# Holding batch 1's V, its spreads and its global casts behind batch 0's copies of V, and counting instruction fetches longer, in a planned attention and MoE kernel

## The chip, the core and the metric

The kernel runs on one core of one Trainium2 chip. A core has TensorE (PE, matmuls; PEld is its weight load), VectorE (DVE), ScalarE (ACT), GpSimd (POOL) and SyncE (SP), each with an instruction queue of its own that runs in order, and 16 DMA engines that all queues share. SP, ACT and POOL issue transfers; one that changes the type of its data is issued by POOL. The metric is device time in microseconds (us) of a whole execution; the median of three runs of the kernel before is 330.26 us (330.26 to 330.88).

## The reference

Eight batches of attention with eight heads of 64, a local part of 512 tokens with a band of 32 to each side, and 32 global tokens; then a two-layer MoE expert on all 4352 rows.

```
k_all = concat(k_g, k_l);  v_all = concat(v_g, v_l)
out_g = softmax(q_g k_all' / 8) v_all                     # 32 global rows see all 544 keys
s_ll  = where(|i - j| <= 32, q_l k_l' / 8, -1e9)          # local rows see a band
out_l = softmax(concat(q_l k_g' / 8, s_ll)) v_all         # and the 32 global keys
x     = concat(out_g, out_l), heads side by side          # 4352 x 512
h     = x @ w_in                                          # 512 -> 2048
out   = (h * clip(h + 3, 0, 6) / 6) @ w_out               # 2048 -> 512, float32
```

## The kernel before

**A planner writes the order.** Every piece of work is an `Op` with its engines and their estimated costs, the operations that it depends on, and the buffers that it takes and frees. It stands in a named stream; within a stream the order is fixed. `Plan.lay` (L123) keeps a clock for each engine and lays, step by step, the operation that can start first; among those that can start on one engine within 0.03 us the lowest rank of its stream wins. An operation with a choice of engines goes to the one on which it ends first. The order that comes out is what each engine's queue executes; on the chip only semaphores hold an engine. So a changed rank or cost moves instructions, and nothing else.

**Instruction fetches.** The planner counts PE instructions in blocks of 256 (`BLOCK`, L43). When PE passes a block's edge, the next block is taken to arrive at `fetched` (L180): 3.4 us later, and up to 3.0 us more where the DMA clock lies ahead. An operation that would run into a block not yet there gets 20 added to its rank (L147), so that others go first.

**Attention of a batch.** `loads` (L407) brings q and k, `g_first` (L461) the global q and k of batches 0 and 1, `v_loads` (L536) V. `turn_qk` (L597) transposes them on DVE (`qt`, `kt`; L609, L614, L624), after which small copies called halos (L631, stream "kg", on POOL or ACT) repeat edge columns. `local` (L697) makes a pair of 32-row windows of all heads, four pairs a batch: scores on PE (L731 or, from batch 2 on, L718), mask and maximum on DVE (L762), exponential on ACT (L768), turning on PE (L777), its copy out of PSUM (L319 on ACT, L321 on DVE), the product with V on PE (L795), normalising and transposing on DVE (L804, L805, L818). `globe` (L822) does the same for the global rows (L843, L850, L855, L866, L876).

**Copies of V.** The product with V needs the rows of V shifted by 32 and beside the global rows of V. `v_loads` loads V into `v0` and shifts it with copies within the chip ("strips", L538 to L568, stream "vs"): about 29 for batch 0, on POOL, ACT or DVE; ten for each later batch, on POOL alone. The global V is loaded into `vg` by `vg_load` (L517) and repeated into `vs` by four transfers of SP (`spread`, L526). `made["strips"]` keeps batch 0's strips.

**The global q and k** go as FP32 into a staging tile and are cast into `gn0`. For batch 0, `once` (L486) loads 32 rows once and casts them four times into four quarters of the partitions. For batch 1, `g_first` loads them four times for q and four times for k (eight transfers of SP into `graw`) and casts each in one instruction (L479, ACT or DVE).

**The MoE.** `moe_first` (L971) multiplies by `w_in` (L926), gates on ACT and DVE (L937, L933); `moe_second` (L992) multiplies by `w_out` (L953), copies out (L961) and stores by SP. Batch 0's first layer goes in parts of 128, 128 and 256 columns (`PARTS`). The attention of batch b lies beside the MoE of batch b - 1. `w_out` comes in four transfers of POOL, `load_w_out` (L588).

**Order of the loads.** All transfers of stream "l0" keep their order on POOL: batch 0's, `w_in`, batch 1's q and k, batch 1's global V and V, `w_out`, then batch 2's q and k (`rawq`, `rawk`). Further, the planner lets no engine have more than eight transfers under way (`LANES`, L98).

Of the kernel before, what the change touches and what calls it, by code (L numbers as in the profile page):

```python
# [9 lines left out]
FP32 = mybir.dt.float32  # L10
# [27 lines left out]
class Plan:  # L38
# [5 lines left out]
    FETCH = 3.4  # L44
    COLD, SLOW = 30.0, 1.9
    SWITCH, ALONE = 0.097, 0.0
    SPARE, PHASES = 0.4, 9
# [75 lines left out]
    def lay(self):  # L123
        at = self.at = {n: 0 for n in self.streams}
        clock = {}
        order = []
        total = sum(len(s) for s in self.streams.values())
        while len(order) < total:
# [46 lines left out]
            if e == "PE":  # L175
                wait, when = self.stalls(op, start, self.cost(op, e, start))
                end += wait
                self.mode = op.mode[1]
                if self.count % self.BLOCK + op.n >= self.BLOCK:
                    self.fetched = when + wait + self.FETCH + min(3.0, max(0.0, clock.get("DMA", 0.0) - when - 0.5))  # L180
                self.count += op.n
# [12 lines left out]
def kernel(  # L194
# [12 lines left out]
    nc = tc.nc  # L207
# [51 lines left out]
    graw = tiles("graw", 2, [P, NC, D], FP32)  # L259
# [37 lines left out]
    for name, rank in (("l0", 0), ("ld", 5), ("lq", -2), ("sh", 0), ("sq", 0), ("st", 2), ("g0", 0), ("ga", -9), ("first", -9), ("pad", -30), ("gc", -6), ("gd", 3), ("cast", -5), ("msk", lambda n: 1 if n < 9 else 1.25), ("tq", lambda n: 0 if n < 8 else 3), ("kg", -1), ("vs", 2.2), ("clr", 1),  # L297
                       ("s", 0.5), ("mx", lambda n: 1.2 if n < 33 else 2.7), ("ex", 1.2), ("t", -0.5), ("etc", 0), ("av", -0.7), ("nm", 1.5),
                       ("xp", -0.5), ("gx", 1),
                       ("mf", lambda n: 9 + n * 1e-3), ("ms", lambda n: 9 + (n + len(PARTS) * NDFF + 2) * 1e-3), ("t1", 0), ("gate", -0.7), ("ot", 0)):  # L300
        plan.stream(name, rank)
# [159 lines left out]
    def g_first(b):  # L461

        after = [w_in_l[1][1]] if b else []
        state[b]["gl"] = {}
        for k, src, name in ((1, k_g, "k"), (0, q_g, "q")):
            if b == 0:
                once(k, src, name)
                continue
            rows = src[b].rearrange("(c e) g d -> e g c d", e=2)
            g, w, got = Buf("gn" + name, 1), Buf("gr" + name, 1), []  # L470
            state[b]["gn", k] = g
            for e in range(2):
                for f in range(2):
                    got.append(load("sh" if b else "ga" if k else "g0", "SP" if b or not k else "ACT", 0.47, 0.2, graw[k][quarter(e, f)], rows[e], after, () if got else [w]))

            def cast(engine, k=k):
                o, i = (t[k].rearrange("p c d -> p (c d)") for t in (gn0, graw))
                if engine == "ACT":
                    nc.scalar.copy(out=o, in_=i)  # L479
                else:  # L480
                    nc.vector.tensor_copy(out=o, in_=i)
            op = Op({"ACT": 0.37, "DVE": 0.3}, None, got, [g], [w])
            op.emit = lambda op=op, cast=cast: cast(op.engine)
            state[b]["gl"][k] = [plan.add("gc", op)]

    def once(k, src, name):  # L486

        raw_ = ots[k][0:W].rearrange("g (h d) -> g h d", d=D)
        got = load("ga", "ACT", 0.47, 0.3, raw_, src[0].rearrange("h g d -> g h d"))
        state[0]["gn", k] = Buf("gn" + name, 1)  # L490
        state[0]["gl"][k] = []
        for e in range(2):
            for f in range(2):
                def cast(engine, e=e, f=f):
                    o, i = gn0[k][quarter(e, f)], raw_.rearrange("g (c e) d -> g e c d", e=2)[:, e]
                    if engine == "ACT":
                        nc.scalar.copy(out=o, in_=i)
                    else:
                        nc.vector.tensor_copy(out=o, in_=i)
                op = Op({"ACT": 0.37, "DVE": 0.3} if k else {"ACT": 0.37}, None, [got], [state[0]["gn", k]] if not state[0]["gl"][k] else [])  # L500
                op.emit = lambda op=op, cast=cast: cast(op.engine)
                state[0]["gl"][k].append(plan.add("gc" if k else "gd", op))
# [23 lines left out]
    def spread(b, units_, after):  # L526
# [3 lines left out]
        for u in units_:  # L530
            a = ORDER[u].index("g") * W
            st["vs"][u, 0] = [load("sh", "SP", 0.5, 0.3, lambda u=u, a=a: vs[v.slot][a:a + W, u],
                                lambda: vg[v.slot][0:W].rearrange("p (j h) d -> p j h d", j=1).to_broadcast([W, NJ, H, D1]), [after], lat=2.0 + LATE[b])]
            st["vs"][u, 1] = list(st["vs"][u, 0])

    def v_loads(b, to):  # L536
# [6 lines left out]
        vl = [load(to, "POOL", 0.8, 1.05 if b else 1.25, lambda j=j: v0[v.slot][:, j, :, 0:D],  # L543
                   v_l[b, :, j * P:(j + 1) * P, :].rearrange("h s d -> s h d"), lat=LATE[b] if b else 3.3 - 0.4 * j) for j in range(NJ)]

        def shift(u, z, n, src, js, dj, need):
# [8 lines left out]
            op = Op({"POOL": c, "ACT": c, "DVE": c if n == W else 1.35 * c} if b == 0 else {"POOL": c}, None, [vl[j + dj] for j in js])  # L555
# [457 lines left out]
    with tc.manual_schedule():  # L1013
# [14 lines left out]
        w_out_l = load_w_out()  # L1028
        for b in range(2, B):
# [23 lines left out]
        moe_second(B - 1, NJ - 1, 2)  # L1053
        for need, op in made["strips"]:
# [41 lines left out]
```

## Time and profile before

| | |
|---|---|
| median of three runs | 330.26 us |
| the profiled execution's own time | 331.21 us |
| its span, first to last instruction | 329.4 us |
| busy: PE, DVE, ACT, POOL | 306.1, 259.6, 236.7, 154.7 us |
| PE busy from 0 to 16 us, 16 to 24, 24 to 44 | 6.45, 4.20, 15.80 us |
| PE busy from 44 to 56 us, 56 to 96, 96 to 226 | 11.74, 39.16, 130.00 us |
| mean granted clock of TensorE | 0.988 |

A PE that counts as busy is not at its peak, since the ends of matmuls are modelled; an idle PE, though, is idle. A wait is told as the engine and line that waited, and what released it; "issue" is a wait for nothing that the profile shows. In the timeline a row gives the start, the length, what ran, how many, and in brackets the idle time before it and what ended that.

### The profile page before, as it was taken

What the parts mean: (1) busy time and instruction counts of PE and PEld (TensorE: products, weight loads), DVE (VectorE), ACT (ScalarE), POOL (GpSimd) and SP (SyncE); (2) the same over time, 40 slices, a digit from 0 to 9 for tenths busy, and PEclk for the clock granted to TensorE, in tenths of its full rate; (3) what the DMA queues carried; (4) which work ended last, traced back from release to release, by engine and by line L of the source; (5) the groups of instructions that cost most, each with busy time, mean ns of one, the idle gap of its engine ahead of it and who ended that gap; (6) DMA issues with size and microseconds to landing.
All of it is one profiled execution on the core that took longest, in us unless ns stands there. A gap on an engine that the chain in (4) does not pass through costs nothing.

```text
span 329.4 us, 11223 instructions
## 1 busy us (share of the span) xinstructions
PE 306.1 (93%) x4484; PEld 172.8 (52%) x4484; DVE 259.6 (79%) x916; ACT 236.7 (72%) x545; POOL 154.7 (47%) x201
## 2 busy tenths in 40 slices
PE   4457889999989999999999999999999999999995
PEld 3336786555545555555554554554455545556653
DVE  7789996898878898989899899898898874672210
ACT  7869668757977798769867987589758796553221
POOL 9998299409995802993249519923800000000000
PEclk9977999999999999999999999999999999999999
DMA  8999999999952996299969991998211012101222
GB/s 199 186 207 193 206 210 113 176 251 162 191 106 66 157 178 124 47 134 180 211 88 147 169 131 34 120 190 145 62 39 34 2 34 67 32 2 33 65 57 72
DMA packets 105429, 39.67 MB, mean 120 GB/s; under 512 B 92256, under 2 KB 98144, under 8 KB 105376
## 3 DMA queue, kind: packets, MB, share of 16 engines
q0 software_dynamic: 91392, 16.91, 65.8%
q1 hardware_dynamic: 13440, 21.91, 28.2%
q8 instruction: 35, 0.57, 0.7%
q10 hardware_dynamic: 544, 0.13, 0.2%
q14 instruction: 18, 0.15, 0.1%
HBM read 35.26 MB, written 8.91 MB: 134 GB/s over the span
## 4 chain that ended last, share of the span: by engine, by line
PE 76%; POOL 9%; issue 6%; DVE 4%; ACT 2%; DMA 1%; SPq 0%; POOLq 0%
PE m L953 32%; PE m L926 31%; PE t L777 3%; POOL vs L561 3%; PE a L795 3%; PE s L718 2%; POOL v L309 2%; DMA rawq<-rawq 1%; PE s L835 1%; PE t L866 1%; PE a L876 1%; DVE gts L933 1%; PE s L731 1%; DVE x L805 1%; PE m L731 1%
## 5 line engine op out<-in xcount | busy, mean ns | idle before, releaser
L953 PE MATMUL m<-wout,gts 128*128 128x512 f16 (+1 forms) x560 | 131.8, 373 | 0.0
L926 PE MATMUL m<-xt,win 128*128 128x512 f16 (+2 forms) x640 | 121.6, 339 | 3.3 <-DVE gts L933 3.3
L933 DVE SCALAR_TENSOR_TENSOR gts<-t,m 128x512 f16<-128x512 f32 x136 | 92.0, 681 | 30.5 <-ACT t L937 29.0
L937 ACT ACTIVATE t<-m 128x512 f32<-128x512 f32 x136 | 80.8, 596 | 43.4 <-PE m L926 41.2
L561 POOL COPY vs<-v 32x1056 f32<-32x1056 f32 (+5 forms) x87 | 79.4, 912 | 48.9 <-DMA v<-in_v_l_dram 44.8
L926 PEld LDWEIGHTS <-win 128*128 128x128 f16 x704 | 70.7, 114 | 49.6 <-issue 4.9
L768 ACT ACTIVATE ex<-sm,mx 128x128 f16<-128x128 f32 x256 | 86.3, 395 | 10.1 <-DVE mx L762 9.5
L953 PEld LDWEIGHTS <-gts 128*128 128x128 f16 x560 | 51.2, 98 | 49.8 <-issue 2.4
L762 DVE CUSTOM_DVE_ANT_0 sm<-s,mask 128x128 f32<-128x128 f32 x240 | 56.2, 284 | 8.1 <-PE s L731 3.2
L961 ACT COPY ot<-m 128x512 f32<-128x512 f32 (+1 forms) x35 | 20.0, 572 | 12.6 <-PE m L953 12.6
L319 ACT COPY et<-t 128x1024 f16<-128x1024 f16 x26 | 26.2, 1006 | 3.3 <-PE t L777 3.1
L309 POOL DMA_DIRECT2D v<-in_v_l_dram x32 | 28.2, 900 | 0.0
L309 POOL DMA_DIRECT2D rawq<-in_q_l_dram x12 | 12.6, 1056 | 23.9 <-DVE qt L665 13.0
L805 DVE TENSOR_TENSOR x<-a,rec 128x512 f16<-128x512 f32 x32 | 22.1, 692 | 1.1
L818 DVE STREAM_TRANSPOSE xt<-x 128x512 f16<-128x512 f16 x32 | 22.4, 701 | 0.2
L762 DVE DVE_READ_ACCUMULATOR2_ANT mx<- 128x1 f32 x256 | 21.2, 83 | 0.0
L777 PEld LDWEIGHTS <-ex 128*128 128x128 f16 x256 | 17.4, 102 | 6.3 <-issue 0.4
L777 PE MATMUL t<-ident,ex 128*128 128x128 f16 x240 | 19.2, 225 | 0.0
L795 PEld LDWEIGHTS <-et 128*32 128x32 f16 x1024 | 10.0, 97 | 14.1 <-ACT ex L768 3.8
L665 DVE STREAM_TRANSPOSE qt<-rawq 128x512 f16<-128x512 f16 x24 | 15.8, 687 | 0.6 <-DMA rawq<-rawq 0.6
L795 PE MATMUL a<-vs,et 128*32 128x65 f16 x1024 | 14.2, 196 | 2.0 <-ACT et L319 1.1
L319 ACT COPY etg<-t 128x640 f16<-128x640 f16 x15 | 10.4, 693 | 7.6 <-PE t L866 7.5
(93 smaller groups left out, 220.4 us busy)
## 6 DMA issues: line engine op xcount, KB each, us to landing
out_dram<-ot SPq DMA_DIRECT2D x62, 128.0 KB, 2.4
vs<-vg SPq DMA_DIRECT2D x32, 132.0 KB, 7.6
v<-in_v_l_dram POOLq DMA_DIRECT2D x32, 128.0 KB, 9.1
rawq<-in_q_l_dram POOLq DMA_DIRECT2D x12, 256.0 KB, 5.8
rawk<-in_k_l_dram POOLq DMA_DIRECT2D x12, 256.0 KB, 7.6
rawq<-rawq SPq DMA_DIRECT2D x12, 254.0 KB, 7.1
rawk<-rawk SPq DMA_DIRECT2D x12, 254.0 KB, 7.5
win<-in_moe_w_in_dram POOLq DMA_DIRECT2D x4, 512.0 KB, 10.3
```

The source lines that it names most:

```text
L309: eng.dma_start(out=o() if callable(o) else o, in_=i() if callable(i) else i)
L319: nc.scalar.copy(out=o(), in_=i())
L561: (nc.gpsimd if op.engine == "POOL" else nc.vector).tensor_copy(out=o(), in_=i())
L762: nc.vector.tensor_tensor_reduce(out=sms[sm.slot], in0=scored(c // 2)[:, z:z + P], in1=mask(m), scale=-scale, scalar=3.0e38, op0=ALU.add, ...
L768: nc.scalar.activation(out=exs[ex.slot][:, un, c, :], in_=sms[sm.slot], func=EXP, scale=-1.0, bias=mxs[mx.slot])
L777: nc.tensor.matmul(out=turned(tp)[:, z:z + P], lhsT=exs[ex.slot][:, un, c, :], rhs=ident, is_transpose=True)
L795: nc.tensor.matmul(out=o[hq * W:(hq + 1) * W, 4 * f + 2 * un + kh, 0:D + 1], lhsT=ets[et.slot][:, un, c, quarter(e, f) if b >= WORDS else ...
L805: nc.vector.tensor_tensor(out=xs[x.slot].rearrange("p g (a d) -> p g a d", a=2), in0=o[:, :, 0:D].rearrange("p g (d a) -> p g a d", a=2), ...
L926: nc.tensor.matmul(out=mps[ps.slot][:, k * n:(k + 1) * n], lhsT=column_tile(c)[:, m], rhs=x, start=(m == 0), stop=(m == KC - 1))
L933: nc.vector.scalar_tensor_tensor(out=g, in0=shape(t1s[t1.slot][:, 0:all_]), scalar=1.0, in1=shape(mps[ps.slot][:, 0:all_]), op0=ALU.min, o ...
L937: r = plan.add("t1", Op(("ACT", 0.09 + all_ * 0.00083), lambda: nc.scalar.activation(out=t1s[t1.slot][:, 0:all_], in_=mps[ps.slot][:, 0:al ...
L953: nc.tensor.matmul(out=mps[ps.slot][:, 0:n], lhsT=gfn(c), rhs=w_out_t[c // 4][:, c % 4, cols], start=(c == 0), stop=(c == NDFF - 1))
```

## The change

It has six parts. (1) Batch 1's load of the global V may be laid on POOL only after the last of batch 0's strips has been laid (`holds`); what follows it in its stream (batch 1's V, `w_out`, batch 2's loads) follows it here too. (2) Batch 1's four spreads depend on the third transfer of `w_out`. (3) Batch 1's global q and k go the way of batch 0's: one transfer each into a new tile `graw0`, and four casts each, in a new stream "gp", on POOL or ACT. (4) The fetch of a block is counted as 7.0 us from a start before 40 us and as 5.2 us later, whatever the DMA clock. (5) Ranks: "kg" from -1 to 0.5, "vs" from 2.2 to 1.5, "ex" from 1.2 to 1.9, "nm" from 1.5 to 0.7, "st" from 2 to 3.5, "ot" from 0 to 3; `ALONE` and `SPARE` to 0.5. (6) Costs: strips of batch 0 on POOL and ACT, casts, V's issue, spreads.

```diff
-    FETCH = 3.4
-    SWITCH, ALONE = 0.097, 0.0
-    SPARE, PHASES = 0.4, 9
+    SWITCH, ALONE = 0.097, 0.5
+    SPARE, PHASES = 0.5, 9
...
-                    self.fetched = when + wait + self.FETCH + min(3.0, max(0.0, clock.get("DMA", 0.0) - when - 0.5))
+                    self.fetched = when + wait + (7.0 if when < 40.0 else 5.2)
...
-    graw = tiles("graw", 2, [P, NC, D], FP32)
+    graw0 = tiles("graw0_", 1, [W, 2, H, D], FP32)[0]
...
-    ("st", 2), ... ("kg", -1), ("vs", 2.2), ... ("ex", 1.2), ... ("nm", 1.5), ... ("ot", 0)
+    ("st", 3.5), ... ("gp", 3.9), ... ("kg", 0.5), ("vs", 1.5), ... ("ex", 1.9), ... ("nm", 0.7), ... ("ot", 3)
...
     def g_first(b):
-        after = [w_in_l[1][1]] if b else []
         state[b]["gl"] = {}
         for k, src, name in ((1, k_g, "k"), (0, q_g, "q")):
-            if b == 0:
-                once(k, src, name)
-                continue
-            rows = src[b].rearrange("(c e) g d -> e g c d", e=2)
...
-                    got.append(load("sh" if b else "ga" if k else "g0", "SP" if b or not k else "ACT", 0.47, 0.2, graw[k][quarter(e, f)], rows[e], after, () if got else [w]))
...
-            op = Op({"ACT": 0.37, "DVE": 0.3}, None, got, [g], [w])
...
+            once(b, k, src, name)
-    def once(k, src, name):
+    def once(b, k, src, name):
+        raw_ = (graw0[:, k] if b else ots[k][0:W].rearrange("g (h d) -> g h d", d=D))
+        got = load("sh" if b else "ga", "SP" if b else "ACT", 0.47, 0.45 if b else 0.3, raw_, src[b].rearrange("h g d -> g h d"), [w_in_l[1][1]] if b else ())
...
-                        nc.vector.tensor_copy(out=o, in_=i)
-                op = Op({"ACT": 0.37, "DVE": 0.3} if k else {"ACT": 0.37}, None, [got], [state[0]["gn", k]] if not state[0]["gl"][k] else [])
+                        (nc.gpsimd if engine == "POOL" else nc.vector).tensor_copy(out=o, in_=i)
+                op = Op({"POOL": 0.43, "ACT": 0.42} if b else {"ACT": 0.42, "DVE": 0.4} if k else {"ACT": 0.42}, None, [got], [] if e or f else [g])
...
-            st["vs"][u, 0] = [load("sh", "SP", 0.5, 0.3, ...
+            st["vs"][u, 0] = [load("sh", "SP", 0.5, 0.45, ...
...
-        vl = [load(to, "POOL", 0.8, 1.05 if b else 1.25, ...
+        vl = [load(to, "POOL", 0.88, 1.05 if b else 1.25, ...
...
-            op = Op({"POOL": c, "ACT": c, "DVE": c if n == W else 1.35 * c} if b == 0 else {"POOL": c}, ...
+            op = Op({"POOL": 0.25 + 0.205 * len(js), "ACT": 0.2 + 0.22 * len(js), "DVE": c if n == W else 1.35 * c} if b == 0 else {"POOL": c}, ...
...
         w_out_l = load_w_out()
+        for u in range(NU):
+            state[1]["vs"][u, 0][0].deps[0].deps.append(w_out_l[NDFF // 2])
...
         moe_second(B - 1, NJ - 1, 2)
+        state[1]["g4"].deps[0].holds = {"POOL": made["strips"][-1][1]}
```

The order that the planner then writes differs at these places (read from the two built programs). Batch 0's eight halos are all on ACT (before, four on ACT and four on POOL). Of batch 0's strips 21 are on POOL, 5 on ACT and 3 on DVE (before 17, 4 and 8). POOL issues batch 1's global V and V behind its last strip, then two transfers of `w_out`, four of the new casts, the other two of `w_out`, `rawq`. The other four new casts are on ACT. In the first 44 us DVE loses a cast of q and a copy of turned scores (L321), both to ACT; later it takes over some copies of output (L961) and gives up some of turned scores. On SP, batch 2's first `rawq` copy stands ahead of the first store of output instead of behind it. PE has the same 8970 instructions; their groups are interleaved a little differently from the 840th on.

## Prediction

> **What bounds the kernel now.** I read the page's slices first, then the windows table by stage, then PE's waits, and last the timelines of PE, POOL, SP and DVE in the first 60 us. From the page:
>
> ```profile
> PE   4457889999989999999999999999999999999995
> POOL 9998299409995802993249519923800000000000
> PEclk9977999999999999999999999999999999999999
> ...
> q8 instruction: 35, 0.57, 0.7%
> ```
>
> After the seventh slice PE is never under 8 tenths, and the windows table has it busy 130.00 of 130 us from 96 to 226. There a row of eight 512-column matmuls in the chain takes 1.73 us, 216 ns each: the middle is PE's own work, which the change leaves as it is. What it can move is PE's idle time: 329.4 - 306.1 = 23.3 us, of which 0 to 44 us holds 44 - 6.45 - 4.20 - 15.80 = 17.5. PE's waits up to 60 us:
>
> ```profile
> PE m L731 <- issue: 3.5, 1, 3.5
> ...
> PE m L926 <- DVE gts L933: 3.3, 3, 1.6
> PE m L731 <- POOL kt L631: 1.6, 1, 1.6
> ```
>
> (The rows left out wait for batch 0's first transposes, which the change hardly touches.) PE's timeline shows these waits, and two late in the kernel:
>
> ```profile
> 14.93 1.00 PE L731 MATMUL m<-kt,qt 32*32 32x128 f16 x57 [1.65 <-POOL kt L631]
> ...
> 18.55 0.35 PE L731 MATMUL m<-kt,qt 32*32 32x128 f16 x19
> 22.39 0.83 PE L731 MATMUL m<-kt,qt 32*32 32x128 f16 x45 [3.50 <-issue]
> ...
> 35.32 0.86 PE L926 MATMUL m<-xt,win 128*128 128x128 f16 x12 [0.81 <-DVE gts L933]
> ...
> 54.74 0.29 PE L731 MATMUL s<-kt,qt 32*32 32x128 f16 x12 [0.26 <-issue]
> ...
> 92.57 0.30 PE L795 MATMUL a<-vs,et 128*32 128x65 f16 x16 [0.84 <-POOL vs L561]
> ...
> 230.93 0.24 PE L718 MATMUL s<-kt,qt 64*32 64x128 f16 x6 [0.56 <-issue]
> ```
>
> The stop of 3.50 us is inside a run of equal matmuls whose inputs are there. Adding up the timeline's counts, two instructions for each matmul (weights and product), it comes at 702, the one at 54.74 at 1982, which is five times 256 later, the one at 35.32 at 1214, twice 256 after 702. So PE stops at block edges for instructions; the page's queue q8 moved 35 pieces of 16 KB. The edge before 702 is 446, the 59th matmul of the run that restarts at 14.93, at about 15.5: 22.39 - 15.5 = 6.9 us from edge to next block. The same between 48.4 (edge 1726) and 54.74: 6.3. POOL and SP:
>
> ```profile
> 12.70 0.52 POOL L631 COPY kt<-kt 32x64 f32<-32x64 f32 x2
> 13.17 1.42 POOL L309 DMA_DIRECT2D win<-in_moe_w_in_dram  x2
> 14.65 0.52 POOL L631 COPY kt<-kt 32x64 f32<-32x64 f32 x2
> ...
> 34.19 1.05 POOL L309 DMA_DIRECT2D wout<-in_moe_w_out_dram  x2 [1.88 <-DMA qtmp<-in_k_l_dram]
> ```
>
> The halos that PE awaits at 14.93 stand on POOL behind two issues of `w_in`. k of batch 1 lands at 34.2; q, by the row before, at 31.8. DVE's timeline, then SP's:
>
> ```profile
> 28.78 0.74 DVE L561 COPY vs<-v 32x528 f32<-32x528 f32 x1
> ...
> 35.02 2.11 DVE L609 STREAM_TRANSPOSE qt<-xt 128x1024 f32<-128x1024 f32 x1
> ...
> 39.52 2.06 DVE L614 STREAM_TRANSPOSE kt<-qtmp 128x256 f32<-128x256 f32 x4
> ```
>
> ```profile
> 34.26 2.52 SPq L309 DMA_DIRECT2D vs<-vg  x4
> ```
>
> DVE copies a strip of V while PE starves, and transposes q and k of batch 1 late; SP issues batch 1's four spreads at 34.26.
>
> **The change, part by part.** Sums are made against the profiled execution (331.21 us: span 329.4 and 1.8 around it), which is 0.95 above the median of 330.26.
>
> *Halos to ACT.* ACT's halos are 243 ns. In the new order ACT's last cast of k moves from 9.15 to 8.9 (two casts of 0.41 fewer ahead of it, 0.53 more for the one from DVE); with it (0.52) come two exponentials (0.69), a cast (0.41), four halos (1.0), a cast and a strip (0.8) and four halos (1.0), to 13.3. So the run of 14.93 starts 1.6 earlier. Behind it come four strips (1.6) and six exponentials (1.9): 16.8, where before they were done at 15.7, so turning, second scores and the first product with V come about 1.1 later (19.4 for 18.2). That costs nothing as long as the block stop covers it: edge 446 passes at 13.9, the block comes 6.9 later, at 20.8. Gain there 1.6, ends 0 (the stop ends when DMA pleases) and 1.6.
>
> *DVE's stretch, 23.3 to 44.2.* DVE is busy 19.41 of 20 us from 24 to 44, and its transposes of batch 1 hold the gates. It loses two strips (0.43, 0.74) and a copy (0.45), 1.6 us. But the transpose of q now stands before two gates, and q lands near 31.8 at the earliest; with ACT's five exponentials ahead of its first gate, DVE idles about 1.4 us before. Following the rows (q 31.7 to 33.6, two gates 34.9, normalising 35.8, k 37.9, five gates, a normalising and a transpose to 42.3, `gn` 43.0) the first scores of batch 1 start at 43.3 instead of 44.50, with 24 instead of 20 matmuls of 108 ns done before them. Worth 1.2 + 0.43 = 1.6 in all, and this contains the 1.6 of the halos: the second gain mostly goes into the wait for q. Ends: 0 and 3.2 (both add).
>
> *Batch 1's V and spreads later.* POOL's last strip of batch 0 ends near 27.6 (before 30.97), V's issue (3.51) at 31.7. Its place in the transfers is the same, behind k, which lands at 34.2; so `w_out` isn't late. Nothing, if POOL stays ahead of that; POOL waits for DVE's k until 41.65 before. The four casts on POOL, not in the trace: between 0.39 and 0.70 each (copies of 264 and 528 columns), 1.6 to 2.8 us; they end before 35, when the third `w_out` could go anyway. The spreads are another matter: four SP issues, 2.5 us, now behind the third `w_out`, which I put at 45.8: issued near 34.0, and the page's median of 11.8 to landing. The eight spreads up to 60 us took 6.6 to 13.0 us from issue to landing, median 7.4, so the last, issued by 48.3, is in at 54.9 to 61.3. The first product of batch 1 stood at 57.91, behind a group of scores (0.67) that now follows it: at 57.24, and less the 1.6 at 55.6. It may wait 0 to 5.7; I take 0.4, near the median landing (55.7). Everything on PE stands behind it; SP holds `rawq` behind them, due far later (69).
>
> *Fewer small transfers of global q and k.* Eight SP issues (5.3 us) become two; the casts leave DVE or ACT no more than they take. 0.
>
> *Fetches counted longer.* I add durations per block in both orders (from the chain's rows: four 512-column matmuls 0.86, eight turns 0.45, 64 scores 0.67; 32 products with V 0.36 by the timeline's starts). The block from 1726 falls from 5.8 to 5.0 us of work while the fetch took 6.3: the stop at 1982 grows by 0.6 (0 to 0.8). The block that ends at the stop of 230.93 (27 edges after the first, some ten instructions early) grows from 5.8 to 8.9: that stop goes, -0.6 (0 to -0.6).
>
> *Batch 2's strips.* At 92.57 PE waited for the last of them. POOL now issues `rawq`, then three instead of four loads of V before the first strips, 0.88 less, and the new order has these 0.9 us ahead: -0.8 (0 to -1.0). What is late next is ACT's copy, which ended before.
>
> *Other places of the middle* are new interleavings, which a planner can miss: +0.3, ends -0.5 and +1.5.
>
> Sum: -1.6 + 0.4 + 0.6 - 0.6 - 0.8 + 0.3 = -1.7, or 329.5 for the profiled execution. From the median 330.26: **328.6 us**.
>
> **The rivals.**
>
> *The spreads come too late (other side).* For: their landing reached 13.0 us, and they now compete with batch 2's `rawq` pieces. It eats the whole gain from a wait of 2.1, which is a landing after 9.4 us. At 13.0 the wait is 5.7: 330.26 - 2.1 + 5.7 = 333.9; at 11 it is 3.7, and the time 331.9. Against: `w_out` has no spreads beside it before 45. Chance 0.18, time 331.9.
>
> *ACT becomes the bound of the front.* ACT gets 2.0 us of halos and strips ahead of the exponentials and later five exponentials before the first gate. If the stop at 702 ends when it did, ACT's 1.1 us are uncovered and the DVE gain is lost to waits: front +0.5 instead of -1.6, so 330.26 - 1.7 + 2.1 = 330.7. Chance 0.11.
>
> *The stops are not fetches.* Then the 3.50 lasts up to 22.39 whatever comes before; the front's 1.6 and the 0.6 at 230 are not won, the 0.6 is not lost: 330.26 - 0.8 + 0.4 + 0.3 = 330.2. The spacing of 256 speaks against it. Chance 0.06. The Trainium skill, "Runtime: NRT & Kernel Launch", section "Instruction fetch mechanics", has this rule: instructions come in 16 KiB blocks fetched while the current one executes, at a cost "mostly hidden". By that rule the stop of 3.50 us should not be there; the block size agrees with this trace, the hiding does not.
>
> *Clock.* Between 22.4 and 26 the granted clock was 0.50. PE had 3.11 us of work in it. Half of that is the price either way; the new idle stretches (14.3 to 16.9, 20.1 to 20.8) are of the same kind: inside the range, no case of its own.
>
> **How the numbers follow.** My forecast has 0.65, with its own range 326.5 to 330.0 (below: the front at -3.2 without waits; above: most of the front's gain lost). Late spreads have 0.18, ACT 0.11, no fetches 0.06. A measurement of this kernel tells about 0.2%, 0.66 us, from no change. Faster (under 329.6): 0.60 of the forecast's, 0.01 of ACT's, 0.02 of no fetches': 0.63. Same (329.6 to 330.9): 0.05, 0.02 of the spreads', 0.05 of ACT's, 0.03: 0.15. Slower: 0.16 of the spreads', 0.05, 0.01: 0.22. The range takes the forecast's and reaches into late spreads, 326.3 to 332.0.
>
> **What would show it.** Right: PE's wait on POOL's halos gone; the stop in the second unit-pair ends near 20.8; first batch-1 scores near 43.3; no wait of L795 on POOL near 90; no stop near 230. Wrong: a wait of L795 for DMA of `vs` near 56, a stop at 1982 of over 1 us, a DVE wait for `xt` of more than 2 us, or new PE waits between 60 and 280.

## The result, and the profile after

The changed kernel takes 327.87 us (median of 20 runs, 326.62 to 330.61), the kernel before beside it 330.52 (20 runs, 328.99 to 332.56): a ratio of 0.9921, 95% interval 0.9902 to 0.9941. That is 2.6 us less, where 1.7 were forecast. The profiled execution of the kernel after took 328.56 us with a span of 326.8; its span is 2.6 below the 329.4 of before. One profile of the experiments, that of four halos back on POOL, is of an execution that took 521.50 us, with a granted clock of 0.56 from 28 us on, so only what lies ahead of 28 us is read there. From the page of the kernel after:

```profile
PE   4477898799999999999999999999999999999995
POOL 9999999029955935665009944963900000000000
PEclk9999999999999999999999999999999999999999
...
q8 instruction: 35, 0.57, 0.7%
```

PE's eighth slice now has a 7 where the kernel before had a 9: the time won ahead of it is already spent there. The granted clock is at full speed in every slice, while before it was 0.50 from 21.3 to 28.2 us. PE's waits say what the eighth slice holds (columns: wait in all, times, longest):

```profile
PE m L934 <- issue: 1.8, 1, 1.8
...
PE m L907 <- DVE gts L914: 1.2, 1, 1.2
PE m L907 <- issue: 1.0, 2, 0.7
PE s L712 <- issue: 0.9, 1, 0.9
PE m L712 <- issue: 0.3, 1, 0.3
```

PE's wait for POOL's halos is gone, the stop of 3.5 in the second unit-pair is 0.3, and there is a new stop of 1.8 within a row of products with `w_out`. The two stops of L907 are at edges 958 and 1214 (0.30 and 0.67). PE's timeline after:

```profile
12.82 1.12 PE L712 MATMUL m<-kt,qt 32*32 32x128 f16 x60
...
19.15 0.63 PE L776 MATMUL a<-vs,et 128*32 128x65 f16 x32 [1.08 <-ACT et L318]
19.71 0.50 PE L712 MATMUL m<-kt,qt 32*32 32x128 f16 x19
20.51 0.83 PE L712 MATMUL m<-kt,qt 32*32 32x128 f16 x45 [0.29 <-issue]
...
42.37 0.73 PE L712 MATMUL s<-kt,qt 32*32 32x128 f16 x64
...
52.89 0.30 PE L712 MATMUL s<-kt,qt 32*32 32x128 f16 x13 [0.92 <-issue]
...
55.40 0.42 PE L776 MATMUL a<-vs,et 128*32 128x65 f16 x32
...
59.09 1.25 PE L934 MATMUL m<-wout,gts 128*128 128x512 f16 x5 [1.85 <-issue]
...
91.36 0.42 PE L776 MATMUL a<-vs,et 128*32 128x65 f16 x32
```

Line by line against before: the 3.50 stop that ended at 22.39 ends at 20.51. The first scores of batch 1 stand at 42.37 instead of 44.50 (forecast 43.3). The stop at edge 1982 is 0.92 instead of 0.26, the first product of batch 1 with V stands at 55.40 and waits for nothing, the products of 91.36 no longer wait for POOL's strips, and no stop is left near 230. The stop at 59.09, at edge 2238, is new. POOL and SP after, then DVE:

```profile
12.61 2.14 POOL L308 DMA_DIRECT2D win<-in_moe_w_in_dram  x3
19.71 0.77 POOL L308 DMA_DIRECT2D xt<-in_q_l_dram  x1
...
23.91 3.78 POOL L542 COPY vs<-v 32x528 f32<-32x528 f32 x6
28.22 3.51 POOL L308 DMA_DIRECT2D v<-in_v_l_dram  x4
```

```profile
33.96 2.71 SPq L308 DMA_DIRECT2D vs<-vg  x4
```

```profile
30.82 0.15 DVE L832 TENSOR_SCALAR mx<-top 128x1 f32<-128x1 f32 x1
31.08 2.08 DVE L590 STREAM_TRANSPOSE qt<-xt 128x1024 f32<-128x1024 f32 x1
```

POOL's last strip of batch 0 ends at 27.6, as forecast. The four spreads leave at 33.96, where they left at 34.26 before: the dependency on `w_out` orders the planner's clock, and no semaphore stands for it on the chip. DVE's transpose of q starts 0.11 after DVE is free.

**Where the 2.6 us are.** I add up the time that each matmul takes in an unbroken row (0.216 us for one of 512 columns), in each kernel's order, and compare when the same amount of PE work has been done (work in us, time before, time after, difference):

```
work   before   after   after - before
   4    15.46   13.46    -2.00   the halos
  18    42.37   39.75    -2.62
  28    52.67   50.17    -2.50   end of the front
  30    55.19   53.34    -1.85   behind edge 1982
  34    59.36   59.53    +0.17   behind edge 2238
  60    85.88   85.81    -0.06
  70    97.33   96.34    -0.99   behind batch 2's strips
 190   221.88  220.61    -1.27
 200   233.07  230.82    -2.25   behind the stop near 230
 290   324.98  322.47    -2.50
```

So in these two profiles the front wins 2.5 and all of it is handed back at two block edges by 60 us. What reaches the end is won later: 0.9 at the strips, 1.0 at the stop of 230, and about 0.8 in small steps. That is read from the two traces; no run undoes the strips' part or the stop's alone. A part of the small steps shows in the groups by line of the stretch from 62 to 270 us, of before and then of after (count, busy us, mean ns and idle us before them):

```profile
L926 PE MATMUL m<-xt,win 128*128 128x512 f16 x384 | 90.6, 380 | 0.0
```

```profile
L907 PE MATMUL m<-xt,win 128*128 128x512 f16 x384 | 89.3, 380 | 0.0
```

The same 384 products with `w_in` are busy 1.3 us less, but only a part of that is time won. By the records of PE they stand in rows that break 40 times in before and 34 times in after, and the last product of a row counts with its full 380 ns, the others with the 216 to the next. From each product's start to the start of the next matmul on PE it is 0.6 us less in all.

### The profile page after: what moved, and what is told of

Read it like the earlier page. It is cut to its first block, busy times and chain, and to the rows that moved or that the text cites. A ratio compares the mean times of both kernels' runs of the same rounds, so it can differ in the third digit from the quotient of the medians.

```text
span 326.8 us, 11215 instructions
## 1 busy us (share of the span) xinstructions
PE 305.8 (94%) x4484; PEld 172.8 (53%) x4484; DVE 258.4 (79%) x913; ACT 238.3 (73%) x550; POOL 157.7 (48%) x205
## 4 chain that ended last, share of the span: by engine, by line
PE 86%; POOL 5%; DMA 3%; DVE 2%; issue 2%; ACT 0%; POOLq 0%
PE m L934 37%; PE m L907 35%; PE t L758 4%; DMA xt<-in_q_l_dram 3%; PE a L776 3%; PE s L699 3%; PE t L847 1%; POOL vs L542 1%; PE s L816 1%; POOL v L308 1%; PE a L857 1%; PE s L712 1%; POOL win L308 1%; DVE qt L590 1%; DVE kt L595 1%
## 5 line engine op out<-in xcount | busy, mean ns | idle before, releaser
L907 PE MATMUL m<-xt,win 128*128 128x512 f16 (+2 forms) x640 | 121.0, 338 | 2.2 <-DVE gts L914 1.2
L907 PEld LDWEIGHTS <-win 128*128 128x128 f16 x704 | 70.4, 114 | 48.0 <-issue 3.8
L542 POOL COPY vs<-v 32x1056 f32<-32x1056 f32 (+4 forms) x91 | 81.7, 898 | 29.1 <-DMA v<-in_v_l_dram 24.8
L749 ACT ACTIVATE ex<-sm,mx 128x128 f16<-128x128 f32 x256 | 84.9, 394 | 7.2 <-DVE mx L743 6.5
L318 ACT COPY et<-t 128x1024 f16<-128x1024 f16 x28 | 28.1, 1005 | 8.1 <-PE t L758 8.0
L308 POOL DMA_DIRECT2D v<-in_v_l_dram x32 | 28.2, 896 | 0.0
L942 ACT COPY ot<-m 128x512 f32<-128x512 f32 (+1 forms) x29 | 16.5, 570 | 15.3 <-PE m L934 15.2
L743 DVE DVE_READ_ACCUMULATOR2_ANT mx<- 128x1 f32 x256 | 21.3, 83 | 0.0
L758 PE MATMUL t<-ident,ex 128*128 128x128 f16 x240 | 19.9, 225 | 1.5 <-ACT ex L749 1.5
L318 ACT COPY etg<-t 128x640 f16<-128x640 f16 x16 | 11.1, 692 | 10.5 <-PE t L847 10.5
L650 DVE STREAM_TRANSPOSE kt<-rawk 128x512 f16<-128x512 f16 x24 | 15.5, 679 | 0.0
## 6 DMA issues: line engine op xcount, KB each, us to landing
win<-in_moe_w_in_dram POOLq DMA_DIRECT2D x4, 512.0 KB, 11.3
```

Of the source, the lines that this page charges most:

```text
L308: eng.dma_start(out=o() if callable(o) else o, in_=i() if callable(i) else i)
L318: nc.scalar.copy(out=o(), in_=i())
L542: (nc.gpsimd if op.engine == "POOL" else nc.vector).tensor_copy(out=o(), in_=i())
L743: nc.vector.tensor_tensor_reduce(out=sms[sm.slot], in0=scored(c // 2)[:, z:z + P], in1=mask(m), scale=-scale, scalar=3.0e38, op0=ALU.add, ...
L749: nc.scalar.activation(out=exs[ex.slot][:, un, c, :], in_=sms[sm.slot], func=EXP, scale=-1.0, bias=mxs[mx.slot])
L758: nc.tensor.matmul(out=turned(tp)[:, z:z + P], lhsT=exs[ex.slot][:, un, c, :], rhs=ident, is_transpose=True)
```

## The experiments

Twelve kernels were run. Eight of them edit the order that the planner has laid, in place: an operation gets another engine or an added small transfer or copy, or `move(op, ahead_of)` takes it out of the list and puts it ahead of another, so that nothing else changes its place. In the code, "..." marks lines left out. Two (old fetch, no hold) plan anew, one changes a count, one is the kernel after once more.

**Four halos back on POOL.**

```diff
+for h, at in ((state[0]["halo"][1], w_in_l[0][1]), (state[0]["halo"][3], w_in_l[2][1])):
+    h.engine = "POOL"
...
+    move(h, at.deps[0])
```

> The changed kernel (327.87 us, span 326.8), with four of batch 0's eight halos back on POOL, behind the issues of w_in, as they stood before; nothing else moves. Edge theory: PE's second run of scores starts near 14.9 us instead of 12.8, edge 446 passes at 15.5 instead of 13.5, so the block at 702 comes at 22.4 instead of 20.5 and the first scores of batch 1 at 44.0 to 44.4 instead of 42.37. The front loses 1.6 to 2.0 us; total 328.0 to 329.9, depending on whether the stop of 1.85 us at 59.09 stays. Rival (ACT was the bound of the front, and DVE's relief made the gain): ACT has 1.0 us less to do, the stop at 702 may move, the first scores of batch 1 stay at 42.4 or come earlier; total 327.9 or less.

Measured: 328.82 us, ratio to before 0.9941 (0.9923 to 0.996), against 0.9921 for the kernel after. PE's timeline ahead of 28 us:

```profile
14.96 1.01 PE L712 MATMUL m<-kt,qt 32*32 32x128 f16 x57 [1.66 <-POOL kt L612]
...
22.57 0.83 PE L712 MATMUL m<-kt,qt 32*32 32x128 f16 x45 [2.59 <-issue]
```

The wait for POOL is back, and with it the stop: it ends 2.06 later than in the kernel after (20.51), as the run that passes edge 446 starts about 2 later. So the halos own 2.0 us of the front up to there; the first scores of batch 1 lie behind what can be read. The median of the whole rises by 0.95, with intervals that overlap a little.

**Halos on ACT in the kernel before**, the same part alone, from the other side.

```diff
+for h in state[0]["halo"]:
+    h.engine = "ACT"
```

> The kernel before, with batch 0's four halos of POOL on ACT at the place that the order gives them, and nothing else moved. Theory (the block edge sets the front): the run of matmuls that waited for POOL until 14.93 starts 1.3 to 2 earlier, the stop of 3.50 ends 1.3 to 2 earlier, about 20.7, and up to 1 us of it reaches the end, because DVE's 1.6 us of strips still hold the gates and the stops later give back what is early: time 329.3 to 330.5. Rival (the stop ends when the transfers of that time allow it): the stop grows to 5 us, ends at 22.4, time 330.5.

Measured: 329.68 us, ratio 0.9974 (0.9957 to 0.999), 0.9 less than before. PE's timeline:

```profile
13.55 1.01 PE L731 MATMUL m<-kt,qt 32*32 32x128 f16 x57 [0.23 <-ACT kt L631]
...
20.85 0.83 PE L731 MATMUL m<-kt,qt 32*32 32x128 f16 x45 [1.67 <-issue]
...
42.99 0.73 PE L731 MATMUL s<-kt,qt 32*32 32x128 f16 x64
...
230.88 0.24 PE L718 MATMUL s<-kt,qt 64*32 64x128 f16 x6 [1.51 <-issue]
```

The stop ends 1.54 earlier, so it follows its edge and not the transfers: the rival falls. The granted clock was at full speed throughout the front here, as in the kernel after, and still batch 1's scores come only 1.51 earlier than before (42.99 for 44.50): what the stop gave, and nothing more for the clock. By equal work this kernel stays 1.55 ahead of before up to 72 us and is 1.0 ahead at 221; then the stop that was 0.56 in before is 1.51 and ends at 230.88, in before at 230.93. The profiled execution (span 329.3, and with 331.15 us the longest of the ten) keeps nothing, the median 0.9. So in this execution a gain in the front was collected 200 us later by a block edge.

**Strips and a copy back on DVE.**

```diff
+for op, at in ((strips[-5], state[0]["xT", 0]), (strips[-4], state[0]["xT", 2]),
+               (state[0]["globe"][0][1], plan.streams["mx"][33])):
+    op.engine = "DVE"
+    move(op, at)
```

> The changed kernel with two strips of V (0.43 and 0.74 us) back on DVE ahead of its first gates and the copy of turned scores (0.45) back on DVE ahead of the second maximum; nothing else moves. Theory (DVE is the bound from 24 to 44 us): 1.6 us more on DVE, of which 0.82 fits into its idle time before the first gate, so the transposes of batch 1's q start near 31.9 instead of 31.08, the first scores of batch 1 near 43.2 instead of 42.37, total 328.7. Rival (q's landing is the bound there, DVE had room): both times stay within 0.2 us, total 327.9.

Measured: 327.82 us, ratio 0.9911 (0.9883 to 0.9939): no difference to the kernel after. By equal work it is 0.85 later from the very first matmuls on, which the edit doesn't touch, and 1.7 later from 34 us on, so the edit costs about 0.85 there, by one profile of each. Behind edge 2238 it is 0.49 ahead, for PE runs through that edge without a stop:

```profile
57.95 1.90 PE L934 MATMUL m<-wout,gts 128*128 128x512 f16 x8
```

So DVE's relief is about half of the 1.6 that the forecast counted, and worth nothing at the end.

**Batch 2's V held until 58 us**, with a two-element copy on POOL that waits for a transpose of batch 1.

```diff
...
+at = laid.index(state[1]["xT", 0]) + 1
+laid[at:at] = [Op(("POOL", 0.1), lambda: nc.gpsimd.tensor_copy(out=peek, in_=xts[state[1]["xt"].slot][0:1, 0, 0:2]))] + loads_
```

> The changed kernel with batch 2's V held on POOL by a small copy that reads batch 1's first transposed output (56.95 us), so that its five transfers are issued near 57.7 to 62 instead of 53.3 to 57.4; nothing else moves. Theory (a block's fetch is as slow as the transfers beside it; the stop of 1.85 us at 59.09 is the fetch begun at edge 1982, 52.9 us, among V's small pieces): the block comes near 57.0, the stop falls to under 0.5 us, total 326.1 to 326.6. Rival (the stop is only the order: 4.4 us of work between two edges): stop of 1.85 us stays, total 327.9. If V is late for its strips, at 77 us, a wait of POOL for V shows there.

Measured: 327.74 us, ratio 0.9912 (0.9886 to 0.9939). PE's timeline:

```profile
58.00 1.25 PE L935 MATMUL m<-wout,gts 128*128 128x512 f16 x5 [0.75 <-issue]
```

The stop shrinks from 1.85 to 0.75, which is neither of the two expectations, and the median doesn't move by more than it can tell.

**Batch 1's V ahead of POOL's last six strips**, the hold undone in place.

```diff
+last = [op for _, op in made["strips"] if op.engine == "POOL"][-6]
+for d in [state[1]["g4"]] + state[1]["v0"]:
+    move(d.deps[0], last)
```

> The changed kernel with batch 1's global V and V issued ahead of the last six strips of batch 0 on POOL, as they stood before; nothing else moves. Theory: the last strip ends at 31.7 us instead of 27.6, the product with V of batch 0's fourth pair waits from 30.78 to about 31.9, and since DVE waits for batch 1's q beside it, little of it is left: first scores of batch 1 0 to 0.6 us later, total 327.9 to 328.5. Rival (the hold is the main gain of the change): the first scores of batch 1 go back to 44 us or more, total 330 or more.

Measured: 327.46 us, ratio 0.9903 (0.9866 to 0.994). The strips now make PE wait (`vs` of POOL, 1.8 us in all, three times), which reaches batch 1's scores as 0.43; behind edge 2238 the kernel is 1.24 ahead, with a stop of 0.47 there. So the hold itself, as a place on POOL, brings nothing.

**A real wait for the spreads**: SP reads two elements of the third `w_out` tile first.

```diff
...
+nc.sync.dma_start(out=peek, in_=w_out_t[2][0:1, 0, 0:2])
+spread_now()
...
```

> The kernel after, with one small SP transfer that reads the third w_out tile put ahead of batch 1's four spreads: the wait that the planner counts becomes a wait on the chip. Theory (in the kernel after nothing holds the spreads, which leave at 33.96 as soon as vg is there, so the late-spreads rival could not happen): here they leave at 43 to 46 and land 7 to 13 us later, the first product of batch 1 with V (55.40 in the kernel after) waits for vs by 0 to 4 us; time 328 to 331. Rival (the hold was there and cost nothing): spreads leave where they left, 33.96, and the time stays at 327.9.

Measured: 328.05 us, ratio 0.9929 (0.9909 to 0.9948). SP, then PE:

```profile
43.68 0.72 SPq L1059 DMA_DIRECT2D peek<-wout  x1
44.51 2.63 SPq L309 DMA_DIRECT2D vs<-vg  x4
```

```profile
56.21 0.43 PE L777 MATMUL a<-vs,et 128*32 128x65 f16 x32
56.57 0.74 PE L713 MATMUL s<-kt,qt 32*32 32x128 f16 x64
57.24 1.90 PE L935 MATMUL m<-wout,gts 128*128 128x512 f16 x8
```

With a wait on the chip the spreads leave 10.5 us later, and the product with V still waits for nothing (56.21, at once behind what stands ahead of it). So the first half of the theory holds, that nothing held them before; of the second, a wait of 0 to 4 us, nothing came. The stop at 1982 grows to 1.36, the one at 2238 disappears, and there is one of 0.51 at 227.03, at the edge of the stop near 230 in before. PE's order is that of the kernel after, which runs through that edge; by the records of PE and q8 the next block landed there 7.5 us after PE entered the one before it, and 5.5 in the kernel after.

**Global q and k of batch 1 loaded twice**, into rows of two tiles that nobody uses then.

```diff
...
+for spare, src in ((ots[2], k_g), (t1s[2], q_g)):
+    nc.sync.dma_start(out=spare[0:W].rearrange("g (h d) -> g h d", d=D), in_=src[1].rearrange("h g d -> g h d"))
```

> The kernel after, with the global k and q of batch 1 loaded a second time, into unused rows of two other tiles: the number of small pieces beside batch 1's q and k goes back to that of the kernel before. Theory (fewer small pieces let q land 0.7 earlier, and the front gained 0.9 more than forecast by it): q's transpose starts at 31.7 to 32.0 instead of 31.08 and the first scores of batch 1 at 43.0 to 43.4 instead of 42.37; time 327.9 to 328.8. Rival (q's landing differs from one execution to the next, or follows w_in alone): transpose at 31.1 and time 327.9.

Measured: 328.37 us, ratio 0.9941 (0.9913 to 0.9968). DVE's timeline:

```profile
30.70 2.08 DVE L590 STREAM_TRANSPOSE qt<-xt 128x1024 f32<-128x1024 f32 x1
```

q is there by 30.70 with all the small pieces back, so they were not what held it. What differs from before is q's issue on POOL: 20.33 there, 19.71 in the kernel after and 19.70 here, since halos no longer stand ahead of it. But the issue alone doesn't fix the landing. In two executions of the kernel after (19.71 and 19.76) it came 11.3 and 9.8 us after the issue, at 31.05 and 29.60, and here 10.3 after it: it differs from one execution to the next, as the rival has it. The 0.5 us in the median lies within both intervals and isn't seen in this profile (0.56 ahead of the kernel after at the end), so what it is stays open.

**Sixty-eight warm-up matmuls instead of a hundred.** They have no part in the output.

```diff
-    for _ in range(100)], [clean],
+    for _ in range(68)], [clean],
```

> The kernel after, with 68 instead of 100 warm-up matmuls at PE's start, which are over long before the first input lands; nothing else moves, but every block edge of 256 instructions lies 32 matmuls later in the work. Theory (the stops are fetches of instruction blocks): the edge once at 13.48 is passed at about 17.4, the next block is there 7 us later, and the stop moves from after 19 matmuls of the run of 64 to after 51, and lasts till about 24.3: 3 to 4 us there; the stop after three of eight products with w_out near 58 moves as well. Time 328.5 to 331, by how much later waits take in. Rival (the stops are not fetches, but tied to a place in the work or to a time): the stop stays after 19 matmuls, 0.3 long, and the time at 327.9.

Measured: 328.94 us, ratio 0.9957 (0.9932 to 0.9982), PE's timeline:

```profile
19.79 0.93 PE L712 MATMUL m<-kt,qt 32*32 32x128 f16 x51
23.21 0.40 PE L712 MATMUL m<-kt,qt 32*32 32x128 f16 x13 [2.49 <-issue]
```

The stop moved by exactly the 32 matmuls left out, from behind the 19th to behind the 51st, and is 2.49 long. It ends 5.9 us after its edge (17.27), where 7 were expected. It hangs on the count of instructions and on nothing in the work: the stops are fetches. The Trainium skill, "Runtime: NRT & Kernel Launch", section "Instruction fetch mechanics", has blocks of 16 KiB, and this agrees with 256 instructions to a block and with q8's 35 pieces; that the fetch is "mostly hidden" doesn't agree with 2.49 and 3.50.

**The kernel after once more**, and three further kernels beside it.

> The kernel after, with nothing changed, for a second profile. Theory (the length of a block stop differs from one execution of the same program to the next): the same first batch-1 scores to within 0.5 us (42.1 to 42.9), but stops at edges 1982, 2238 or late in the kernel that differ from 0.92, 1.85 and 0 by 0.5 us or more at one edge at least; median 327.5 to 328.2. Rival (the stop of 1.85 at 2238 belongs to the order of the kernel after): 1.85 within 0.3 again.

Measured: 327.64 us, ratio 0.9914 (0.9899 to 0.9929). PE's timeline:

```profile
26.72 0.27 PE L907 MATMUL m<-xt,win 128*128 128x128 f16 x2 [0.94 <-issue]
...
52.89 0.30 PE L712 MATMUL s<-kt,qt 32*32 32x128 f16 x13 [1.06 <-issue]
...
59.09 1.25 PE L934 MATMUL m<-wout,gts 128*128 128x512 f16 x5 [1.84 <-issue]
```

My theory of stops that differ by chance falls for edges 1982 and 2238, as far as two executions can tell. PE comes to the first of these two 0.14 earlier than in the other execution and leaves both at the same hundredth. So these stops belong to this order and its transfers. Elsewhere the fetch does differ. At the edge passed at 219.4 the next block landed 5.5 us after PE's entry in one execution and 3.2 in the other, both in time; and the stop at edge 958 is 0.94 here and 0.30 there, ending at 26.72 and 26.69.

**The old fetch formula in the kernel after, planned anew.**

```diff
-self.fetched = when + wait + (7.0 if when < 40.0 else 5.2)
+self.fetched = when + wait + 3.4 + min(3.0, max(0.0, clock.get("DMA", 0.0) - when - 0.5))
```

> The kernel after, with only the planner's formula for a block fetch put back to 3.4 plus up to 3.0 of transfers still under way; the order is the same up to the 26th us or so and differs behind it on every engine. Theory (the front up to 20.5 us, which this order shares, makes the gain, and the longer count is worth at most the 0.6 of the stop at 230): 327.3 to 328.8. Rival (the longer count is what makes the gain): 329.5 to 331.

**No hold and no dependency, planned anew.**

```diff
-        for u in range(NU):
-            state[1]["vs"][u, 0][0].deps[0].deps.append(w_out_l[NDFF // 2])
...
-        state[1]["g4"].deps[0].holds = {"POOL": made["strips"][-1][1]}
```

> The kernel after, planned without the hold of batch 1's V behind batch 0's strips and without the spreads' dependency on the third w_out. POOL's and PE's orders differ from about the 20th us on. Theory (neither makes the gain, which comes from the halos and strips that leave POOL and DVE, and from the stops): 327.3 to 328.8. Rival (the hold, or the dependency, makes it): 329.5 to 331.

Measured: 329.99 us, ratio 0.9992 (0.9972 to 1.0011) with the old formula, and 330.41 us, ratio 1.0003 (0.9989 to 1.0018) with no hold and no dependency. My theory fell both times: without either, nearly the whole gain is gone. By equal work against the kernel after, both are 1.1 to 1.3 late at 52 us, win that back at edge 2238 (0.6 and 0.4 ahead behind it), and then lose 3.0 and 2.4 between 60 and 290 us. The groups of 62 to 270 us, of the old formula and then of no hold:

```profile
L907 PE MATMUL m<-xt,win 128*128 128x512 f16 x384 | 90.4, 380 | 1.4 <-DVE xt L799 1.0 <-DVE gts L914 0.2
```

```profile
L907 PE MATMUL m<-xt,win 128*128 128x512 f16 x384 | 91.2, 380 | 0.3
```

The old formula's order has a wait of 1.0 for DVE and 1.1 more busy time in the products with `w_in` than the kernel after (89.3), the other 1.9 more, with 0.3 of idle time before them. From start to start, as above, the products take 1.0 and 1.4 more. So without either of the two named parts the gain is gone, though not by what they say: V's place on POOL is worth nothing by itself, and the dependency isn't a wait. What they change is the planner's clocks, and the order of batches 1 to 7 that comes out with them has fewer hold-ups. Three things were not tested: the hold and the dependency apart, the new ranks and costs alone, and whether any other disturbance of the plan would lose as much.

**Both edits to V together**, as a faster kernel.

> Both edits to V's loads in one kernel: batch 1's V ahead of POOL's last six strips of batch 0, and batch 2's V behind the first transpose of batch 1's MoE input. Theory (each took about 1.2 us off the stop at edge 2238 in its profile, from two sides): stop at 2238 under 0.4, front later by 0.4, time 326.6 to 327.4, ahead of the kernel after. Rival (the stops differ from execution to execution and neither edit does anything): 327.6 to 328.1.

Measured: 328.48 us, ratio 0.9932 (0.9919 to 0.9945), 0.8 slower than the kernel after beside it. PE, then DVE:

```profile
73.92 1.02 PE L908 MATMUL m<-xt,win 128*128 128x512 f16 x4 [1.17 <-DVE gts L915]
```

```profile
72.58 0.71 DVE L651 STREAM_TRANSPOSE kt<-rawk 128x512 f16<-128x512 f16 x1 [1.60 <-DMA vs<-vg]
```

The stop at 2238 is gone, as expected, and behind it PE is 1.22 ahead of the kernel after. (It comes to edge 1982 0.8 late; the granted clock was 0.50 from 28.3 to 31.8 in this profile.) At 72 us DVE waits 1.60 for transfers before it can turn batch 2's k, the gates queue behind that, and PE is 0.18 behind the kernel after from then on. That the late V took its time from transfers that DVE needs is not shown: with the late V alone DVE turns the same k at 71.03 without a wait, and one thing that differs is that SP issues the second part of k at 63.47 here and at 61.06 there. No kernel here is clearly faster than the kernel after.

**The fetch behind edge 1982** decides what the front is worth. From the records of the transfers and of PE: when PE enters the block of 1982, when the 16 KB piece of the next block has landed, how long that is, when the first transfer of batch 2's V (the global V) is issued, and the stop at 2238.

```
kernel                 enters   landed   took   V issued   stop at 2238
loaded twice            52.56    56.94   4.38    52.75      1.56
after                   52.90    57.67   4.77    53.30      1.85
after once more         52.90    57.58   4.68    52.80      1.84
late V of batch 2       52.91    56.62   3.71    58.41      0.75
early V of batch 1      53.03    56.46   3.43    53.40      0.47
halos in before         53.20    55.26   2.06    55.90      none
both edits              53.70    55.97   2.27    59.21      none
real spread wait        53.71    56.17   2.46    53.17      none
strips on DVE           54.43    56.94   2.51    54.65      none
before                  54.74    56.93   2.19    57.33      none
```

Of these ten, who enters before 53.1 has the next block after 3.4 to 4.8 us, who enters later after 2.1 to 2.5; PE goes on 1.4 us after the landing in the kernel after. The kernel after comes to this edge 1.8 us earlier than before and gets the block 0.7 later; the halos in before come 1.5 earlier and get it 1.7 earlier. So the time of entry alone does not decide it. The two kernels planned anew, with other orders, enter at 54.02 (old formula: 3.4 us, and a stop of 0.92) and at 53.43 (no hold: 2.4 us, no stop). Up to 53 us the queues of most of these kernels move batch 2's q and k in pieces of under 512 B, and in the kernel after V's pieces follow at once. The view of transfers from 50 to 60 us of after, and from 52 to 62 of before, 2 us later as its PE is:

```profile
DMA packets 10117, 1.79 MB, mean 179 GB/s; under 512 B 9969, under 2 KB 9969, under 8 KB 10114
```

```profile
DMA packets 5086, 1.28 MB, mean 128 GB/s; under 512 B 4911, under 2 KB 4911, under 8 KB 5082
```

Twice the pieces beside the longer fetch: that was my reason for the late V. It isn't enough. Late V takes about 1.0 off the fetch at the same entry, but early V of batch 1 takes 1.3 off with batch 2's V issued at the same time as in the kernel after. And by the records of the transfers, in the first 2 us of the fetch 1,084 pieces of POOL's queue a us started in the kernel after (4.77), but 902 with the real spread wait (2.46) and 1,012 with the halos in before (2.06). Among the five that enter before 53.1 the same count does put the fetches in order: 698 a us with 3.43, 811 with 3.71, then 984 with 4.38, 1,044 with 4.68 and 1,084 with 4.77. Among the five that enter later it does not: 295 to 1,012 a us, all with 2.1 to 2.5. What makes these fetches long is therefore open; shown is only which kernels have them, and that the kernel after has them in two executions.

## Why the prediction was right, and where it was not

- **Halos to ACT, 1.6 of the front.** Right in kind and nearly in size: 2.0 with the halos taken back, 1.5 with them alone (the edge passes at 13.6, not at 13.9). Shown from both sides by the two runs on halos. That the stop follows its edge is shown by these and by the 68 warm-up matmuls; the rival that the stops are no fetches falls.
- **DVE's stretch, nothing beyond the 1.6.** Mis-sized: the front won 2.5. The step that failed is "q lands near 31.8 at the earliest". It landed at 31.05 and 29.60 in two executions of the kernel after, and DVE began its transpose as soon as it was free, to about 0.1 us. About 0.6 of that is its earlier issue on POOL, which the halos no longer stand in front of; the rest is the time from issue to landing, which differs from one execution to the next. The clock, at 0.50 from 21.3 to 28.2 before and at full speed after, is no rival for the gain: it was at full speed with the halos alone too, which brought batch 1's scores 1.51 forward, no more than the stop's 1.54.
- **Batch 1's spreads, +0.4, and the rival that they come too late.** The step "four SP issues, now behind the third `w_out`" failed: they are behind it in the planner alone. Made real, the wait costs nothing at the product with V, so the rival fails twice. The term of 0.4 measured 0.
- **ACT as the bound of the front** did not come: the first product with V waits 1.1 for ACT at 19.15, and the stop behind it still ends 1.9 earlier.
- **The stop at 1982, +0.6.** Measured 0.65 by equal work. The stop itself is 0.92, and 1.06 in the second execution, just over the 1 us that was named as a sign of being wrong.
- **The stop at 230, -0.6**, and **batch 2's strips, -0.8.** Measured -1.0 (the stop itself was 0.56) and -0.9, by equal work. That the longer block ends the stop holds for the kernel after, where the next block lands within it; with the real spread wait, in the same order, it landed 7.5 us after the entry, and a stop of 0.51 came back.
- **The rest of the middle, +0.3.** Mis-sized, and the step that failed most: a new stop at 2238 cost 2.0, and small steps elsewhere gave about 0.8. The block from 1982 to 2238 has 4.4 us of work in both orders, and I counted a stop only where a block's work changed. So the step that failed is that an edge with unchanged work behind it costs nothing. The fetch took 2.2 us in before and 4.8 after, with PE entering that block 1.8 us earlier; why it took longer is open.

So the sum of -1.7 came near the measured -2.6 with its largest term in the wrong place, and that it came near is luck: the front's gain does not reach the end in the profiled execution, and the end's gain is the middle's. The rest of the middle, put at +0.3, took 2.0 at one edge and gave 0.8 elsewhere. Why this order of the middle is the better one is read from the traces and not isolated by a run.

## What to carry to other kernels

A gain ahead of a block edge counts only after the next edges have been gone through one by one: for each, how much work lies up to the next, and which transfers run while its block is fetched. A line added to a planner is not yet a wait on the chip, and may work through the order alone; an edit in place and a plan made anew answer different questions, and both are needed. An instruction that leaves a queue also moves the transfers issued behind it.

## What the runs showed of the hardware

- Not only semaphores hold PE: with its inputs there it stood up to 3.50 us at the edge of a block of 256 instructions. At one and the same edge (1982) the next block had landed 2.06 to 4.77 us after PE entered the block before it, in ten profiles; the number of small pieces started beside it orders the five that enter first, and not all ten.
- A stop can end at the same time although PE comes to it earlier: at 230.93 in before and 230.88 with the halos on ACT, where PE came 1.0 earlier, and at 52.89 in both executions of the kernel after, where it came 0.14 earlier in one. At the stop of 22.39 it was otherwise: PE passed the edge 446 1.4 earlier and the stop ended 1.54 earlier.
- Thirty-two warm-up matmuls fewer, at a time when PE has nothing else to do, cost 1.1 us in the medians and 0.7 by equal work in the profiles, with nothing else in the order changed.
- One and the same load landed 11.3 us after its issue in one execution of a kernel and 9.8 in another.
